# Expert stage's pools in another order in SBUF, and another order of products in the last gated group

## The chip, the core and the metric

The kernel runs on one core of a Trainium2 chip. The metric is the device time of one execution in microseconds (us). Engines are named as the profile names them: PE (TensorE, matmuls), PEld (its weight loads), ACT (ScalarE), DVE (VectorE), POOL (GpSimd) and SP (SyncE, which issues most DMAs). Every engine works through its own list of instructions in order; semaphores hold an instruction until what it needs is there.

## The reference, cut to what matters

Three stages follow each other on 2304 tokens of 512 features.

```
# attention: 4 batches x 8 heads, 576 tokens, head size 64
proj = x @ w_phi;  proj -= max(abs(proj));  phi(x) = [exp(proj), exp(-proj)]
kv, z = phi(k).T @ v, sum(phi(k));  out = (phi(q) @ kv) / (phi(q) @ z + 1e-6)

# experts: each token goes to one of 8
e_idx = argmax(x @ w_gate + modality_bias[modality_id]);  gate_w = softmax value of e_idx
out[mask_e] = gate_w * (relu(x[mask_e] @ w1[e]) @ w2[e])        # 512 -> 1024 -> 512

# gated layer
out = ((x @ w_a) * (x @ w_b)) @ w_out                           # 512 -> 1536 -> 512
```

## The kernel before

All matmuls run on fp32 values split into a high and a low part, three matmuls for each product (`mm3`, lines 53 to 56), so every weight and every input needs a high copy (made by ACT) and a low copy (high subtracted, made by DVE).

**Attention** (class `Attn`) goes through eight pairs of heads (units 0 to 7). Its order on PE is written by hand (`manual_schedule`). Units 0 to 3 are route 0 (half of the tokens), 4 to 7 route 1. Names: `pjp` projections, `df` differences, `qtp` and `qts` turned queries, `kxp` and `kx` key sums, `nmp` numerators, `x` the result, which `store` writes to the DRAM tensors `xs`; `lgp` are the router's logits, added up by POOL (lines 259, 261).

**Routing** (class `Route`, one for each half): gate (`modi` is its first DVE instruction, line 357), rank, place and table. Its products are `idx`, which tells a gather which rows of `xs` belong to which tile (line 504), `perm`, the way back, and `meta`, which expert a tile belongs to. Route 0 is worked out during attention; route 1 waits for unit 7 and runs on DVE beside the first expert tiles.

**Expert stage** (class `Moe`): four tiles of 608 tokens, two from each half (tile 0 and 1 of route 0, tile 2 and 3 of route 1). For a tile POOL issues five gathers (`xg`, line 561, buffers from the pool `m_xg`), PE turns the gathered rows (`mxt`, line 573), ACT and DVE split them (`mxh`, `mxl`, lines 576 and 577, pool `m_xt`). SP loads eight raw weight pieces (`s`, line 544, pool `m_st`), ACT and DVE split each (`wh`, `wl`, lines 552 and 553, pool `m_w`). Then come eight `l1` steps (`hp`, with `hh` and `hl` as the split result, lines 590 and 591) and four `l2` steps (`yp`, copied to `y`, line 603). A tile has 384 matmuls on PE, 192 of `hp` and 192 of `yp`.

**Conversion**: the gated layer's weights come as 64-bit floats. Ten of their twelve pieces are converted beside the expert stage (`prep` and `narrow`, lines 678 to 718): SP loads `raw` (line 685), ACT, POOL (line 690) and DVE (lines 691 to 698 and 707 to 716) turn it into sums and split parts, SP stores them to the DRAM tensors `wsc`. They have a low priority in the scheduler.

**Gated layer** (class `Moe2`): 36 groups, three pairs of token blocks by twelve slices of 128 columns. A group computes seven products `abp` (line 837), which ACT copies to `pc` (line 839), DVE combines and multiplies (`gate`, lines 825 to 829: `ca`, then `gh` by ACT and `gl` by DVE, first for part 0, then for part 1). The output product (`outp`, line 805) of a group is six accumulations `op0` to `op5`, three matmuls each; `op0` to `op2` need part 0 of the gate, `op3` to `op5` part 1. The products of a group are interleaved with the `op` of the group before. After the twelfth slice `finish` (line 785) scales each accumulation to `o` and POOL scatters it to the output (line 797).

What sets the order: in attention and in the gated layer PE's list is written by hand. In the expert stage a scheduler sets every engine's list when the program is built, from its own costs and from when buffers become free. A pool gives its tiles fixed addresses; pools opened with `side="right"` lie one after the other from the right end of SBUF, in the order in which they are opened, and a tile whose address was another tile's before waits for that one's last reader. Attention has two pools there, for the loaded queries and keys (`a_ld`, 18432 bytes of each partition) and for `df` (`a_df`, 20480 bytes left of it). The free part left of them begins 38912 bytes from the right end.

Of the kernel before, what the change touches and what calls it, by code (L numbers as in the profile page):

```python
# [43 lines left out]
XG = 5  # L44
# [4 lines left out]
def f32(ap):  # L49
    return ap.bitcast(F32)  # L50


def mm3(nc, out, lh, ll, rh, rl, start, stop):
    nc.tensor.matmul(out, lh, rh, start=start, stop=False)  # L54
    nc.tensor.matmul(out, lh, rl, start=False, stop=False)  # L55
    nc.tensor.matmul(out, ll, rh, start=False, stop=stop)  # L56


class Attn:
    def __init__(self, nc, tc, ctx, cst, qk, v, vt, xs, lgp):  # L60
        self.nc, self.tc = nc, tc
        self.qk, self.v, self.vt, self.xs = qk, v, vt, xs
        self.cst, self.lgp = cst, lgp
        pool = lambda n, b, **kw: ctx.enter_context(tc.tile_pool(name=n, bufs=b, **kw))
        self.p_ld = pool("a_ld", 2, side="right")
        self.p_df = pool("a_df", 5, side="right")
        self.p_v = pool("a_v", 3)
        self.p_x = pool("a_x", 2)
        self.p_sm = pool("a_sm", 4)
        self.p_kx = pool("a_kx", 2)  # L70
        self.p_qt = pool("a_qt", 11)
        self.p_vt = pool("a_vt", 2)
        self.p_kp = pool("a_kp", 4)
        self.p_kt = pool("a_kt", 3)
        self.ps_p = pool("aps_p", 2, space=PSUM)
        self.ps_q = pool("aps_q", 2, space=PSUM)
        self.ps_c = pool("aps_c", 2, space=PSUM)
        self.u = {}
# [441 lines left out]
class Moe:  # L520
    NJ = 8

    def __init__(self, nc, tc, ctx, cst, xs, wm, y, ps_l, ps_t):
        self.nc, self.tc, self.cst, self.xs, self.wm, self.y = nc, tc, cst, xs, wm, y
        pool = lambda n, b, **kw: ctx.enter_context(tc.tile_pool(name=n, bufs=b, **kw))
        r = dict(side="right", reuse_waits="tile")
        self.p_st = pool("m_st", 2, **r)
        self.p_w = pool("m_w", 3, **r)
        self.p_xg = pool("m_xg", XG, **r)
        self.p_xt = pool("m_xt", 1, **r)  # L530
        self.p_h = pool("m_h", 1, **r)
        self.ps_l, self.ps_t = ps_l, ps_t

# [121 lines left out]
class Moe2:  # L655
# [124 lines left out]
    def run(self, ws, ts, src0, side):  # L780
        nc, n = self.nc, self.N
        seq = [(p, f) for p in range(NTOK // n // 2) for f in range(self.NF)]
        accs, gs = {}, {}

        def finish(p):
            for m, acc in enumerate(accs.pop(p)):
                bp, b = divmod(2 * p + m // 3, HALF // n)
                if m % 3 == 0:
                    os = self.p_o.tile([P, 3, DM], F32, tag="raw", name="o", bufs=2)
                o = os[:, m % 3, :]  # L790
                c = b * (n // P) + m % 3
                g2 = self.routes[bp].g2[:, c:c + 1]
                if m % 2:
                    nc.vector.tensor_scalar(out=o, in0=acc, scalar1=g2, scalar2=None, op0=ALU.mult)
                else:
                    nc.scalar.activation(o, acc, AF.Copy, scale=g2)  # L796
                st = nc.gpsimd.indirect_dma_start(  # L797
                    out=self.out[:, :],
                    out_offset=bass.IndirectOffsetOnAxis(ap=self.routes[bp].perm[:, c:c + 1], axis=0),
                    in_=o, in_offset=None)  # L800
                for other in self.stores:
                    self.tc.declare_no_dep(st.ins, other, reason="each row of the output is stored once")
                self.stores.append(st.ins)

        def outp(k, m):
            p, f = seq[k]
            if f == 0 and m == 0:
                accs[p] = [self.ps_a.tile([P, 512], F32, tag=f"a{i}", name=f"op{i}") for i in range(6)]
            gh, gl = gs[k]
            wh, wl = ws[k](1536, 512)  # L810
            ms = slice(P * (m % 3), P * (m % 3) + P)
            mm3(nc, accs[p][m], gh[:, m // 3, ms], gl[:, m // 3, ms], wh, wl, f == 0, f == self.NF - 1)
            if m == 5:
                del gs[k], ws[k]
                if f == self.NF - 1:
                    finish(p)

        def stage(k):
            p, f = seq[k]
            ct = lambda tag, shape: self.p_c.tile([P] + shape, F32, tag=tag, name=tag)  # L820
            ca, u, d = ct("ca", [2, n]), ct("u", [2, n]), ct("d", [2, n])
            out = []
            gs[k] = [self.p_g.tile([P, 2, n], F32R, tag=t, name=t) for t in ("gh", "gl")]

            def gate(i, other):
                gh, gl = (x[:, i, :] for x in gs[k])
                nc.vector.tensor_mul(ca[:, i, :], ca[:, i, :], other)  # L827
                nc.scalar.copy(gh, ca[:, i, :])  # L828
                nc.vector.tensor_sub(gl, ca[:, i, :], f32(gh))  # L829

            for i, (col, t) in enumerate(self.PROD):
                ps = self.ps_l.tile([P, 512], F32, tag="l", name="abp")[:, :n]
                wh, wl = ws[k](col, 256)
                th, tl = ts[p][t]
                for c in range(2):
                    cs = slice(P * c, P * c + P)
                    mm3(nc, ps, wh[:, cs], wl[:, cs], th[:, c, :], tl[:, c, :], c == 0, c == 1)
                x = self.p_c.tile([P, n], F32, tag="pc", name="pc", bufs=5)
                nc.scalar.copy(x, ps)  # L839
                out.append(x)  # L840
                if i == 1:
                    nc.vector.tensor_add(u[:, 0, :], x, out[0])
                elif i == 2:
                    nc.vector.tensor_add(ca[:, 0, :], x, out[0])
                elif i == 3:
                    nc.vector.tensor_add(u[:, 1, :], x, u[:, 0, :])
                elif i == 4:
                    nc.vector.tensor_add(d, u, x.unsqueeze(1).to_broadcast([P, 2, n]))  # L848
                elif i == 5:
                    nc.vector.tensor_add(x, x, u[:, 1, :])  # L850
                    gate(0, x)
                elif i == 6:
                    nc.vector.tensor_add(ca[:, 1, :], x, d[:, 0, :])
                    gate(1, d[:, 1, :])
                if k and i > 1:
                    for m in (i - 2,) if i < 6 else (4, 5):
                        outp(k - 1, m)

        src = src0
        self.rest(src, ts[0])  # L860
        for k, (p, f) in enumerate(seq):
            with self.tc.high_priority(offset=-LOWP2):
                for st in side.get(k, ()):
                    st()
            if k + 1 < len(seq) and k + 1 not in ws:
                ws[k + 1] = self.weights(k + 1)
            if f == 0 and p:
                self.rest(src, ts[p])
            with self.tc.manual_schedule(engines={mybir.EngineType.PE}):
                stage(k)  # L870
            if f == self.NF - 2 and k + 2 < len(seq):
                src, ts[p + 1] = self.terms(p + 1, self.p_s)
        with self.tc.manual_schedule(engines={mybir.EngineType.PE}):
            for m in range(6):
                outp(len(seq) - 1, m)


def low(tc, step):
# [171 lines left out]
```

## Time and profile before

| what | value |
|---|---|
| three timed runs | 839.76, 842.74 and 843.46 us |
| the profiled execution | 840.43 us, of which the span from first to last instruction is 838.6 us |
| PE busy | 802.0 us, 96% of the span |
| DVE busy | 595.5 us, 71% |
| ACT busy | 375.1 us, 45% |
| POOL busy | 134.1 us, 16% |
| granted TensorE clock, mean | 0.991 of full speed |

A busy share is a mean over the whole run: attention lasts until about 169 us, the expert stage until about 406 us, and the gated layer from there to the end. The rows below are from single stretches. In a row of the timeline the first number is the start and the second the duration in us; in brackets stands how long the engine had been idle before, and what ended that.

### The profile page before, as it was taken

To read this page: it belongs to the slowest core of one execution; us is meant where nothing else is said; L and a number is where in the kernel's file an instruction comes from. 1 tells how busy PE (TensorE), PEld (TensorE's weight loads), DVE (VectorE), ACT (ScalarE), POOL (GpSimd) and SP (SyncE) were. 2 spreads that over 40 slices of the span, in tenths; PEclk is the share of its full clock that TensorE was granted. 3 is DMA by queue.
4 is the path that set the end of the run, shared out by engine and by line. 5 is a ranking of instruction groups with operands and counts; after the bars stand their busy time and mean duration, and the time that the engine had idled before them with its cause. 6 is when DMAs were issued, how large, how long until landed. Compare 5 with 4: busy or idle time off the path is not lost.

```text
span 838.6 us, 18331 instructions
## 1 busy us (share of the span) xinstructions
PE 802.0 (96%) x7284; PEld 752.8 (90%) x7284; DVE 595.5 (71%) x1071; ACT 375.1 (45%) x665; POOL 134.1 (16%) x164
## 2 busy tenths in 40 slices
PE   9999998899989999989899999999999999999995
PEld 7989888899989999989889899989999999999994
DVE  6877998689995989797588855675554476545553
ACT  4555555434452555444445433553333364333332
POOL 1000018433233522510031000020000002000002
PEclk9999999999998999999999999999999999999998
DMA  8755431667668888776689876576666668666631
GB/s 300 221 173 165 161 90 31 215 217 275 225 202 283 295 303 295 239 288 251 230 286 332 280 241 201 195 257 214 225 202 199 192 201 301 202 203 201 190 135 75
DMA packets 85163, 184.22 MB, mean 220 GB/s; under 512 B 27760, under 2 KB 37520, under 8 KB 85072
## 3 DMA queue, kind: packets, MB, share of 16 engines
q1 hardware_dynamic: 81872, 173.21, 61.6%
q0 software_dynamic: 3040, 9.72, 3.2%
q8 instruction: 58, 0.95, 0.5%
q14 instruction: 33, 0.27, 0.1%
q10 hardware_dynamic: 160, 0.07, 0.0%
HBM read 145.21 MB, written 37.75 MB: 218 GB/s over the span
## 4 chain that ended last, share of the span: by engine, by line
PE 24%; issue 19%; DVE 4%; POOL 2%; ACT 2%; DMA 1%; POOLq 0%; DVEq 0%; ACTq 0%
PE abp L54 5%; PE abp L56 5%; PE abp L55 5%; PE op L56 3%; PE op L55 3%; PE op L54 3%; POOL cvs L690 1%; DMA wsc<-whi 1%; POOL out L797 1%; ACT pc L839 1%; DVE gl L829 0%; DVE d L848 0%; ACT yh L744 0%; DVE ca L827 0%; DVE yl L745 0%
## 5 line engine op out<-in xcount | busy, mean ns | idle before, releaser
L839 ACT COPY pc<-abp 128x384 f32<-128x384 f32 x252 | 120.5, 479 | 199.3 <-PE abp L56 194.2
L54 PE MATMUL abp<-yh,fw 128*128 128x384 f32 x504 | 169.9, 337 | 3.2 <-ACT pc L839 2.2
L55 PE MATMUL abp<-yl,fw 128*128 128x384 f32 x504 | 169.9, 337 | 0.0
L56 PE MATMUL abp<-yh,fw 128*128 128x384 f32 x504 | 169.9, 337 | 0.0
L54 PEld LDWEIGHTS abp<-yh,fw 128*128 128x128 f32 x504 | 94.6, 188 | 13.1 <-ACT pc L839 4.0
L55 PEld LDWEIGHTS abp<-yl,fw 128*128 128x128 f32 x504 | 94.6, 188 | 7.6
L690 POOL TENSOR_SCALAR cvs<-cvs 128x768 f32<-128x768 f32 x24 | 62.7, 2612 | 210.5 <-ACT cvs L689 158.3
L56 PEld LDWEIGHTS abp<-yh,fw 128*128 128x128 f32 x504 | 94.6, 188 | 0.0
L54 PE MATMUL op<-fw,gh 128*128 128x512 f32 x216 | 85.4, 395 | 1.0 <-ACT gh L828 1.0
L56 PE MATMUL op<-fw,gl 128*128 128x512 f32 x216 | 85.3, 395 | 0.9 <-DVE gl L829 0.9
L55 PE MATMUL op<-fw,gh 128*128 128x512 f32 x216 | 85.4, 395 | 0.0
L54 PE MATMUL hp<-mxh,wh 128*128 128x304 f32 x256 | 78.8, 309 | 3.7 <-DVE hl L591 3.7
L55 PE MATMUL yp<-hl,wh 128*128 128x304 f32 x256 | 77.1, 302 | 1.0 <-DVE hl L591 1.0
L55 PE MATMUL hp<-mxl,wh 128*128 128x304 f32 x256 | 77.9, 305 | 0.0
L56 PE MATMUL yp<-hh,wl 128*128 128x304 f32 x256 | 77.7, 304 | 0.0
L56 PE MATMUL hp<-mxh,wl 128*128 128x304 f32 x256 | 77.7, 304 | 0.0
L54 PE MATMUL yp<-hh,wh 128*128 128x304 f32 x256 | 76.7, 303 | 0.5 <-ACT y L603 0.5
L797 POOL DMA_INDIRECT out<-o,perm x18 | 18.1, 1006 | 355.9 <-ACT o L796 349.4
L190 ACT ACTIVATE qts<-qtp 128x512 f32<-128x512 f32 (+1 forms) x80 | 38.3, 557 | 57.2 <-PE qtp L187 57.2
L848 DVE TENSOR_TENSOR d<-u,pc 128x768 f32<-128x768 f32 x36 | 34.4, 956 | 33.9 <-ACT pc L839 33.7
L54 PEld LDWEIGHTS hp<-mxh,wh 128*128 128x128 f32 x256 | 48.7, 191 | 4.9 <-DVE hl L591 2.8
L828 ACT CAST gh<-ca 128x384 fp32r<-128x384 f32 x72 | 36.9, 515 | 34.6 <-DVE ca L827 34.6
(191 smaller groups left out, 1584.4 us busy)
## 6 DMA issues: line engine op xcount, KB each, us to landing
fw<-wsc SPq DMA_DIRECT2D x72, 512.0 KB, 3.6
fw<-wsc SPq DMA_DIRECT2D x144, 256.0 KB, 3.3
raw<-in_moe_w SPq DMA_DIRECT2D x24, 768.0 KB, 6.2
s<-in_moe_w SPq DMA_DIRECT2D x32, 512.0 KB, 5.8
fw<-wsc SPq DMA_DIRECT2D x72, 128.0 KB, 2.6
wsc<-whi SPq DMA_DIRECT2D x12, 640.0 KB, 4.8
wsc<-wsum SPq DMA_DIRECT2D x12, 640.0 KB, 5.0
wsc<-whi SPq DMA_DIRECT2D x12, 512.0 KB, 4.2
```

Source lines behind the costliest of these rows:

```text
L54: nc.tensor.matmul(out, lh, rh, start=start, stop=False)
L55: nc.tensor.matmul(out, lh, rl, start=False, stop=False)
L56: nc.tensor.matmul(out, ll, rh, start=False, stop=stop)
L190: nc.scalar.activation(t[:, s, :n, :], ps[:, :n, :], AF.Exp, scale=1.0 - 2.0 * s)
L690: nc.gpsimd.tensor_scalar(out=s.bitcast(F32), in0=s.bitcast(F32), scalar1=LEAST, scalar2=None, op0=ALU.max)
L797: st = nc.gpsimd.indirect_dma_start(out=self.out[:, :], out_offset=bass.IndirectOffsetOnAxis(ap=self.routes[bp].perm[:, c:c + 1], axis=0), ...
L828: nc.scalar.copy(gh, ca[:, i, :])
L839: nc.scalar.copy(x, ps)
L848: nc.vector.tensor_add(d, u, x.unsqueeze(1).to_broadcast([P, 2, n]))
```

## The change

The first part opens the pools of the expert stage in another order. Bytes from the right end of SBUF, before: `m_st` 0 to 8192, `m_w` to 32768, `m_xg` to 43008, `m_xt` to 62464. Now: `m_w` 0 to 24576, `m_xt` to 44032, `m_xg` to 54272, `m_st` to 62464. So the gather buffers and the raw weights lie in the free part, and the split inputs lie partly where `df` was.

The second part concerns the last of the 36 groups alone: all its seven products are computed without an `op` between them, product 5 ahead of product 4, and then the twelve `op` of the last two groups follow in the order written.

```diff
         r = dict(side="right", reuse_waits="tile")
+        self.p_w = pool("m_w", 3, **r)
+        self.p_xt = pool("m_xt", 1, **r)
+        self.p_xg = pool("m_xg", XG, **r)
         self.p_st = pool("m_st", 2, **r)
-        self.p_w = pool("m_w", 3, **r)
-        self.p_xg = pool("m_xg", XG, **r)
-        self.p_xt = pool("m_xt", 1, **r)
         self.p_h = pool("m_h", 1, **r)
...
-            for i, (col, t) in enumerate(self.PROD):
+            last = k + 1 == len(seq)
+            for i in (0, 1, 2, 3, 5, 4, 6) if last else range(7):
+                col, t = self.PROD[i]
...
-                if k and i > 1:
+                if k and i > 1 and not last:
                     for m in (i - 2,) if i < 6 else (4, 5):
                         outp(k - 1, m)
...
                 stage(k)
+                if k + 1 == len(seq):
+                    for back, m in ((1, 0), (1, 1), (1, 2), (0, 0), (0, 1), (0, 2), (1, 3), (0, 3), (1, 4), (0, 4), (1, 5), (0, 5)):
+                        outp(k - back, m)
...
-        with self.tc.manual_schedule(engines={mybir.EngineType.PE}):
-            for m in range(6):
-                outp(len(seq) - 1, m)
```

The scheduler makes other lists of it on every engine of the expert stage. First place: POOL where attention ends. `xs_63` is route 0's half of the attention result, `idx_2633` its row numbers, `lgp_96` the logits of route 1. Before:

```order
L261 TENSOR_TENSOR lgp_96<-lgp_96,x 128x72
L259 TENSOR_TENSOR lgp_96<-lgp_96,x 128x72
L261 TENSOR_TENSOR lgp_96<-lgp_96,x 128x72
L561 DMA xg<-xs_63,idx_2633 128x512 x4
L561 DMA xg<-xs_63,idx_2633 96x512
L303 IOTA i_3184 128x128
```

Now:

```order
L261 TENSOR_TENSOR lgp_96<-lgp_96,x 128x72
L561 DMA xg<-xs_63,idx_2633 128x512 x4
L561 DMA xg<-xs_63,idx_2633 96x512
L259 TENSOR_TENSOR lgp_96<-lgp_96,x 128x72
L261 TENSOR_TENSOR lgp_96<-lgp_96,x 128x72
L561 DMA xg<-xs_63,idx_2633 128x512 x2
L303 IOTA i_3184 128x128
```

The five gathers of tile 0 now stand ahead of two additions that wait for unit 6. The same place on PE, before:

```order
L211 MATMUL kxp<-v,kt 64x73 x2
L231 MATMUL nmp<-kx,qts 64x73 x32
L187 MATMUL qtp<-ident,df 128x128 x8
...
L211 MATMUL kxp<-v,kt 64x73 x2
L573 MATMUL mxt<-ident,xg 128x128 x8
L231 MATMUL nmp<-kx,qts 64x73 x40
L573 MATMUL mxt<-ident,xg 128x128 x8
L573 MATMUL mxt<-ident,xg 128x96 x4
L54 MATMUL hp<-mxh,wh 128x304
```

Now:

```order
L211 MATMUL kxp<-v,kt 64x73 x2
L573 MATMUL mxt<-ident,xg 128x128 x8
L231 MATMUL nmp<-kx,qts 64x73 x32
L187 MATMUL qtp<-ident,df 128x128 x8
...
L211 MATMUL kxp<-v,kt 64x73 x2
L573 MATMUL mxt<-ident,xg 128x128 x4
L231 MATMUL nmp<-kx,qts 64x73 x40
L573 MATMUL mxt<-ident,xg 128x128 x4
L573 MATMUL mxt<-ident,xg 128x96 x4
L54 MATMUL hp<-mxh,wh 128x304
```

The first eight transposes of tile 0 stand one block of `nmp`, `qtp` and `kxp` earlier, and four more follow ahead of the last `nmp`. On SP the first two weight loads of the stage (`s`) now stand ahead of the stores of units 5 and 6 (before: behind those of unit 6). On ACT `mxh` of the first two blocks now follows the first `wh` (before: the second); on DVE the order is now `wl`, `mxl`, `kx`, `mxl`.

Second place: DVE ahead of route 1's `idx_3959`, on which tile 2 depends. Before:

```order
L503 TENSOR_SCALAR tk<-tbp 128x45
L698 TENSOR_TENSOR wsum<-cvt,cvs 128x768
L591 SCALAR_TENSOR_TENSOR hl<-hp,hh 128x608
L691 TENSOR_SCALAR cvt<-cvs 128x768
L708 TENSOR_TENSOR wsum<-wsum 128x256
L709 TENSOR_TENSOR wsum<-wsum 128x256
L483 TENSOR_TENSOR lhs<-i_3184,cl 128x1152
L493 TENSOR_TENSOR tbqr<-tbqh,tokp 128x9x9 x2
L945 TENSOR_TENSOR top<-meta_2204,meta_3720 1x1
L504 TENSOR_TENSOR idx_3959<-tk,tbp 128x45
```

Now:

```order
L503 TENSOR_SCALAR tk<-tbp 128x45
L464 CAST meta_3720<-meta 1x28
L710 TENSOR_TENSOR wsum<-wsum 128x256
L553 TENSOR_TENSOR wl<-s,wh 128x1024
L591 SCALAR_TENSOR_TENSOR hl<-hp,hh 128x608
L693 SCALAR_TENSOR_TENSOR cvt<-raw,cvt 128x768
L483 TENSOR_TENSOR lhs<-i_3184,cl 128x1152
L493 TENSOR_TENSOR tbqr<-tbqh,tokp 128x9x9 x2
L504 TENSOR_TENSOR idx_3959<-tk,tbp 128x45
```

From `modi` of route 1 to this `idx` DVE's list holds 148 instructions before and 151 now: one `wl`, one `hl`, one L693 and one L710 more, and `top` fewer. On PE 528 `hp` and `yp` matmuls stood ahead of tile 2's first `mxt`, and 552 stand there now: the 24 of one more `l1` step of tile 1. POOL's list there is the same in both: nine conversions (L690) and then the gathers of tile 2.

Third place: ACT in the last gated group. Before:

```order
L839 COPY pc<-abp 128x384 x7
L828 CAST gh<-ca 128x384 x2
L796 ACTIVATE o<-op_16900,g_3960 128x512
L796 ACTIVATE o<-op_16902,g_3960 128x512
L796 ACTIVATE o<-op_16904,g_3960 128x512
```

Now:

```order
L841 COPY pc<-abp 128x384 x6
L828 CAST gh<-ca 128x384
L841 COPY pc<-abp 128x384
L828 CAST gh<-ca 128x384
L796 ACTIVATE o<-op_16900,g_3960 128x512
L796 ACTIVATE o<-op_16902,g_3960 128x512
L796 ACTIVATE o<-op_16904,g_3960 128x512
```

The first `gh` stands ahead of the last `pc`; `o` still stands behind both `gh`. `op_16900` to `op_16905` are the accumulations `op0` to `op5`.

## Rows read from the trace of the kernel before

**Rows 1.** Timeline of PE where attention ends, 153 to 170 us
```profile
153.48 2.25 PE L231 MATMUL nmp<-kx,qts 128*64 128x73 f32 x64 [0.76 <-DVE kx L217]
...
160.53 0.35 PE L211 MATMUL kxp<-v,kt 128*64 128x73 f32 x4 [1.85 <-issue]
...
163.12 3.70 PE L231 MATMUL nmp<-kx,qts 128*64 128x73 f32 x80
...
168.90 0.55 PE L573 MATMUL mxt<-ident,xg 96*128 96x96 f32 x4 [1.05 <-DVE mxl L577]
169.23 0.39 PE L54 MATMUL hp<-mxh,wh 128*128 128x304 f32 x1
```

**Rows 2.** Busy time by stretch: start:end, length, engines (instructions), granted clock, DMA share, GB/s
```profile
160.00:165.00 5.00, 4.47 (x62) 4.06 (x63) 3.84 (x8) 2.42 (x4) 2.08 (x2) 0.67 0.77 222
...
200.00:230.00 30.00, 29.01 (x211) 28.76 (x212) 29.92 (x67) 12.36 (x20) 7.73 (x3) 1.00 0.70 244
...
255.00:260.00 5.00, 5.00 (x30) 5.00 (x30) 0.11 (x1) 0.82 (x2) 1.67 (x2) 0.77 0.87 306
```

**Rows 3.** Timelines of POOL and DVE in the same stretch
```profile
142.31 0.35 POOL L261 TENSOR_TENSOR lgp<-lgp,x 128x72 f32<-128x72 f32 x1
...
151.97 1.11 POOL L561 DMA_INDIRECT xg<-xs,idx  x1 [0.61 <-DMA xs<-x]
...
171.95 0.34 POOL L261 TENSOR_TENSOR lgp<-lgp,x 128x72 f32<-128x72 f32 x1
...
172.32 0.17 DVE L357 SCALAR_TENSOR_TENSOR modi<-lgp,modi 128x9 int32<-128x9 int32 x1 [1.77 <-POOL lgp L261]
```

**Rows 4.** Timelines of DVE, POOL and PE where tile 2 begins
```profile
244.06 0.18 DVE L504 TENSOR_TENSOR idx<-tk,tbp 128x45 int32<-128x45 f32 x1
...
245.74 2.96 POOL L690 TENSOR_SCALAR cvs<-cvs 128x768 f32<-128x768 f32 x1 [5.35 <-ACT cvs L689]
248.85 1.34 POOL L561 DMA_INDIRECT xg<-xs,idx  x1 [0.16 <-issue]
...
253.37 1.09 PE L573 MATMUL mxt<-ident,xg 128*128 128x128 f32 x4 [5.22 <-DMA xg<-xs,idx]
...
259.89 0.79 DVE L591 SCALAR_TENSOR_TENSOR hl<-hp,hh 128x608 fp32r<-128x608 f32 x1 [5.21 <-ACT hh L590]
...
271.54 0.60 PE L573 MATMUL mxt<-ident,xg 128*128 128x128 f32 x4
```

**Rows 5.** Groups of DVE instructions by shape: count, busy us, mean ns, idle before
```profile
L553 DVE TENSOR_TENSOR wl<-s,wh 128x1024 fp32r<-128x1024 f32 x32 | 40.0, 1249 | 3.5 <-ACT wh L552 3.4
...
L591 DVE SCALAR_TENSOR_TENSOR hl<-hp,hh 128x608 fp32r<-128x608 f32 x32 | 24.9, 779 | 10.2 <-ACT hh L590 10.2
...
L693 DVE SCALAR_TENSOR_TENSOR cvt<-raw,cvt 128x768 int32<-128x768 int32 x24 | 22.7, 947 | 0.0
```

**Rows 6.** Timeline of PE: one wait for `hl`, and two matmuls in a row
```profile
204.58 0.41 PE L55 MATMUL yp<-hl,wh 128*128 128x304 f32 x1 [0.99 <-DVE hl L591]
...
405.16 0.30 PE L54 MATMUL yp<-hh,wh 128*128 128x304 f32 x1
405.30 0.30 PE L55 MATMUL yp<-hl,wh 128*128 128x304 f32 x1
```

**Rows 7.** Timelines of SP and PE where the expert stage ends
```profile
387.14 22.42 SPq L727 DMA_DIRECT2D fw<-wsc  x16
...
406.76 0.45 PE L54 MATMUL abp<-yh,fw 128*128 128x384 f32 x1 [1.03 <-ACTq L978]
```

**Rows 8.** Timelines of PE and POOL at the end of the run
```profile
828.04 0.39 PE L56 MATMUL op<-fw,gl 128*128 128x512 f32 x1
...
828.72 0.39 PE L56 MATMUL op<-fw,gl 128*128 128x512 f32 x1
...
827.00 0.97 POOL L797 DMA_INDIRECT out<-o,perm  x1 [126.31 <-ACT o L796]
...
833.37 0.97 POOL L797 DMA_INDIRECT out<-o,perm  x1 [0.30 <-issue]
```

## The prediction

> **What bounds the kernel now.** The page's first part comes first: PE is busy 96% of the span and every other engine has room. So what the change can win lies where PE is idle, where its granted clock is low, or after its last matmul; I went to these places in the timeline. There are three, and DVE, the next busiest engine, decides whether what they give is kept.
>
> Where attention ends, PE waits 0.76 for `kx`, then stands 1.85 at "issue", and 1.05 for `mxl` before the last transposes of tile 0 [rows 1]. The stretch from 160 to 165 is granted 0.67 of the clock [rows 2]; the 80 `nmp` there take 3.70, against 2.25 for 64 (2.8 for 80) a little before [rows 1]. POOL meanwhile: its first gather of tile 0 goes out at 151.97, behind additions that wait for unit 6, although POOL had finished the addition ahead of them at 142.7 [rows 3].
>
> Where tile 2 begins, PE is idle for 5.22, ended by the gather: `idx` was ready at 244.06, POOL finished a conversion at 248.70 before it issued the gather, and 4.52 later (253.37 less 248.85) PE starts [rows 4]. PE arrived at 253.37 less 5.22 = 248.15. Then it is slow: 255 to 260 runs at 0.77 [rows 2].
>
> At the end, six scatters leave POOL one by one, 1.27 apart (827.00 to 833.37 in five steps); the profiled span ends at 838.6, so POOL's chain, not PE's last matmul at 829.1, is what ends last [rows 8].
>
> DVE is busy 29.92 of 30.00 from 200 to 230 [rows 2], while PE waits for `hl` there once, 0.99 [rows 6].
>
> **The change part by part.** All of this is against the profiled time, 840.43.
>
> *Start of the expert stage.* The five gathers of tile 0 move from 151.97 to right behind the addition at 142.31 [rows 3], 1.27 apart as the scatters at the end [rows 8]; with the 4.52 of the gather at tile 2 [rows 4] the first two land by 142.7 + 1.3 + 4.5 = 148.5. The eight transposes that need them then fill the 0.76 gap, and four more stand ahead of the last `nmp`. The wait of 0.76 goes. Behind the last `nmp` eight transposes are left, not twelve (4 x 0.14 = 0.6 less), and the 1.05 wait for `mxl` should mostly go, since three of the five `mxl` now come earlier. That makes the first `hp` 0.76 + 0.6 + 1.05, or about 2.2 earlier than 169.23 where the pieces overlap. But twelve matmuls later (about 170.9) an accumulator is needed that the evictions of the last `nmp` free, and DVE now has a third `wl` (1.25 [rows 5]) ahead of them. I put the lead at 1.4, between 0.2 (that `wl` in the way) and 3.7 (below). Route 1's `modi` hangs on POOL's last addition (171.95), which is itself behind gathers [rows 3]; two of five gathers now go earlier, and I take 2.1 for it.
>
> A place for the rule on the clock: a 0.76 and a 1.85 gap were followed by 0.67 here [rows 1, 2], and a 5.22 gap by 0.77 [rows 2, 4]. [...]
>
> *Tile 2.* Three things meet. Route 1's `idx`: DVE has 151 instructions from `modi` to it and not 148: a `wl` (1.25), an `hl` (0.78), an L693 (0.95) more [rows 5] and an L710 (a third of L693's columns, so 0.3) more; less a short one and the overlap of their starts I take 3.0. So 244.06 - 2.1 + 3.0 = 245.0. POOL: its nine conversions are in the list as before, but the ninth began at 245.74 for a late ACT input [rows 4]; with that input one DVE step earlier it should be done by about 245, and the gather goes out at 245.2 and lands at 245.2 + 4.52 = 249.7. PE: it has 24 more matmuls ahead of this point. At 0.14 each [rows 6] it arrives at 248.15 - 1.4 + 3.4 = 250.1. So the wait goes to about nothing, and with it the low clock. The second transposes for tile 2 stand 90 matmuls on: 250.1 + 0.6 + 90 x 0.14 = 263.3, where before it was 271.54 [rows 4], a lead of 8.2. In parts this is 1.4 from the start, 5.22 of wait, and 1.6 of clock (18.17 from 253.37 to 271.54, where 114 matmuls at 0.14 and one transpose of 0.6 are 16.6).
>
> The rule on the gather: the row says 4.52 from issue to PE's start [rows 4]. [...]
>
> *What is late next.* With PE 8 earlier, DVE has to keep up. Before tile 2's first `hl` it was idle for 5.21 [rows 4]; that was the cover, and the change uses it up. DVE's extra 3.0 is work that the old order did later, so it is not lost, but from there to the end of tile 3 DVE is about as late as PE. I give back 0.9 of the 8.2 (one wait like the 0.99 [rows 6]), which leaves 7.3. The bounds are nothing given back, and everything but the start's 1.4. At the end of the stage the weights for the gated layer (`fw`) are issued from 387.14, and PE began on them at 406.76 [rows 7]; with PE at 399.5 there are 12 us between, so this costs nothing; if it had no cover it would be up to 7.
>
> *The tail.* Of the last group, `op0` now has eight `op` behind it and had five. An `op` takes 0.68 (828.72 less 828.04 [rows 8]), so the first result is ready 3 x 0.68 = 2.04 before its old time against PE's end. On ACT the second `gh` and the last `pc`, which stood between, are done long before; that is worth up to 0.4. PE's amount of work is unchanged. The first three results come 0.68 apart and the rest every 1.36 (two `op`), so the scatters, 1.27 apart, have a stock to draw on: the sixth `op` ends with PE at 829.1, and its scatter's turn is only 2.2 before 833.37, at about 831.2. The gain is 2.2, between 1.5 and 2.6.
>
> Sum: 840.43 - 7.3 - 2.2 = 830.9. The median of the runs shown, 842.74, lies 2.3 above the profiled execution; I take half of this, +1.1, hence 832.0.
>
> **The rivals.** *DVE has no slack*: every us that PE gains in tile 2 is waited out again at `hl` before tile 3 ends. For it: 29.92 of 30.00 [rows 2]. Against it: with DVE that full PE waited once. What stays is 1.4 + 2.2: 836.8, 838.0 at the median's level.
>
> *The start gives more*: PE's clock stays up and the evictions come in time, a lead of 3.7. For it: the filled gap. Against it: the 1.85 stays. PE would then wait at tile 2 for the gather, but all of it would come earlier; the lead at 271.54 is then some 9.5, nothing is given back: 840.43 - 9.5 - 2.2 = 828.7, 829.9 at the median's level. [...]
>
> *Slower*: DVE's new order puts a `wl`, an L693 or a piece of route work right ahead of the `hl` that PE needs, and each of the 16 `hl` of tiles 2 and 3 costs PE a wait of 0.99 [rows 6]. That is 15.8, against 9.5 gained: 846.7, 847.9 at the median's level. It decides from the tenth such wait (9.9 over 9.5). For it: DVE is full, and its order was set by a scheduler with costs of its own. Against it: DVE's idle time ahead of `hl` sums to 10.2 over all 32 [rows 5], so `hl` is mostly early.
>
> *The first part doesn't do what it says*: the gathers go out early but land with the stores and weights of attention's end, so that nothing before `hp` moves; and the new `idx` is later by as much as PE. Only the tail stays: 838.2, 839.4 at the median's level.
>
> **How the numbers follow.** 0.5% of 842.74 is 4.2 us, so faster means under 838.5 and slower over 846.9; less a measurement of this kernel cannot tell from no change. Forecast 0.50, no slack 0.25, more at the start 0.12, slower 0.07, nothing but the tail 0.06. Faster is the forecast, the third case, and half of the second (838.0 lies right at the bound): 0.50 + 0.12 + 0.13 = 0.75. Same is the other half, the last case and a little of the slower one: 0.20. Slower is 0.05. The forecast's own range is 829 to 835 (start 0.2 to 3.7, tail 1.5 to 2.6, the level of the runs 0 to 2.3); the whole range takes in the second and third case and ends short of the slower one: 827 to 840.
>
> **What would show it.** Right: POOL's first five `xg` near 143; first `hp` at 167 to 168; no idle time over 1 us before tile 2's first transposes and granted clock 1.00 in the 15 us after it; the second transposes of tile 2 near 263; `abp` starting near 399.5; the first scatter 6.3 us before the last one still, but starting while PE has over 4 us to go. Wrong: waits for `hl` of about 1 us in a row in tiles 2 and 3; `idx` of route 1 after 247, so that PE waits for the gather as before; a first `abp` at 405 or later; DVE idle for less than 2 us between 250 and 380 with PE waiting for it.

## The result, and the profile after

| | before | after |
|---|---|---|
| median of the timed runs | 840.23 us (837.85 to 843.46, six runs) | 831.11 us (829.97 to 834.64, six runs) |
| span of the profiled execution | 838.6 | 830.2 |
| granted clock, mean | 0.991 | 0.996 |

The ratio is 0.9903, with a 95% interval of 0.9877 to 0.9928. The forecast was 832.0, and the time is inside its own range. The gain is 9.1 us against the median beside it, where the forecast had 10.7 against the median that it knew (842.74); the two repeats below gave 5.9 and 8.1. The places where the time came from are not the ones that I had named, though. I follow PE through the profile after and set it against [rows 1 to 8].

Timeline of PE where attention ends, after (as in rows 1: start, duration, in brackets the idle time before and what ended it):

```profile
153.49 1.09 PE L573 MATMUL mxt<-ident,xg 128*128 128x128 f32 x8
...
162.35 0.66 PE L573 MATMUL mxt<-ident,xg 128*128 128x128 f32 x4 [1.88 <-DVE mxl L577]
162.97 2.76 PE L231 MATMUL nmp<-kx,qts 128*64 128x73 f32 x80
165.66 0.99 PE L573 MATMUL mxt<-ident,xg 128*128 128x128 f32 x8
166.43 0.38 PE L54 MATMUL hp<-mxh,wh 128*128 128x304 f32 x1
...
169.40 0.37 PE L54 MATMUL hp<-mxh,wh 128*128 128x304 f32 x1 [0.91 <-DVE x L242]
```

The eight early transposes fill the gap of 0.76, and the 1.05 for `mxl` is gone. But a new wait of 1.88 stands ahead of the transposes of the third block of rows, and 0.91 ahead of the fourteenth `hp`. The 80 `nmp` took 2.76, not the 3.70 of [rows 1].

Timeline of DVE, after:

```profile
160.47 1.23 DVE L553 TENSOR_TENSOR wl<-s,wh 128x1024 fp32r<-128x1024 f32 x1 [2.80 <-ACT wh L552]
161.61 0.68 DVE L577 TENSOR_TENSOR mxl<-mxt,mxh 128x512 fp32r<-128x512 f32 x1
...
170.32 0.17 DVE L357 SCALAR_TENSOR_TENSOR modi<-lgp,modi 128x9 int32<-128x9 int32 x1 [0.61 <-POOL lgp L261]
...
175.64 0.56 DVE L691 TENSOR_SCALAR cvt<-cvs 128x768 int32<-128x768 int32 x1 [1.85 <-POOL cvs L690]
...
206.06 1.50 DVE L716 TENSOR_TENSOR wsum<-wsum,whi 128x1280 fp32r<-128x1280 f32 x1 [1.10 <-ACT whi L715]
...
248.65 0.19 DVE L504 TENSOR_TENSOR idx<-tk,tbp 128x45 int32<-128x45 f32 x1
```

The 1.88 is in the first two rows: `mxl`, which frees the transposes' accumulator, stands behind a `wl` that waited 2.80 for its `wh`. `modi` is 2.0 earlier than in [rows 3], but `idx` is 4.6 later than in [rows 4]. DVE's wait of 1.85 for `cvs` goes back to a load. ACT in the kernel before, then ACT and POOL after:

```profile
172.38 0.90 ACT L689 ACTIVATE cvs<-raw 128x768 f32<-128x768 f32 x1 [2.41 <-DMA raw<-in_moe_w]
```

```profile
172.47 0.90 ACT L689 ACTIVATE cvs<-raw 128x768 f32<-128x768 f32 x1 [5.15 <-DMA raw<-in_moe_w]
173.46 2.14 POOL L690 TENSOR_SCALAR cvs<-cvs 128x768 f32<-128x768 f32 x1 [3.17 <-ACT cvs L689]
```

POOL waited 3.17 for ACT, and ACT 5.15 for the load of `raw`, which let it begin no earlier than before.

The lead at the first `hp` does not last until tile 2. PE at the 505th of the 1536 `hp` and `yp` matmuls of the stage, before, and then after, with the largest wait ahead of it:

```profile
244.40 0.30 PE L54 MATMUL hp<-mxh,wh 128*128 128x304 f32 x1
```

```profile
217.58 0.41 PE L56 MATMUL yp<-hh,wl 128*128 128x304 f32 x1 [1.08 <-DVE wl L553]
...
244.95 0.30 PE L54 MATMUL hp<-mxh,wh 128*128 128x304 f32 x1
```

There the new order is 0.55 behind.

Timelines of POOL and PE where tile 2 begins, after:

```profile
242.45 2.13 POOL L690 TENSOR_SCALAR cvs<-cvs 128x768 f32<-128x768 f32 x1 [2.86 <-ACT cvs L689]
249.58 2.67 POOL L561 DMA_INDIRECT xg<-xs,idx  x1 [5.00 <-DMA s<-in_moe_w]
252.56 1.54 POOL L561 DMA_INDIRECT xg<-xs,idx  x1 [0.30 <-issue]
254.40 3.60 POOL L561 DMA_INDIRECT xg<-xs,idx  x1 [0.30 <-issue]
258.30 0.94 POOL L561 DMA_INDIRECT xg<-xs,idx  x1 [0.30 <-issue]
...
256.30 0.94 PE L573 MATMUL mxt<-ident,xg 128*128 128x128 f32 x4 [4.26 <-DMA xg<-xs,idx]
...
270.93 0.60 PE L573 MATMUL mxt<-ident,xg 128*128 128x128 f32 x4
```

The conversion is out of the way, as forecast (POOL is idle for 5.00), but PE still waits 4.26. The second transposes of tile 2 stand at 270.93, where [rows 4] had 271.54: by here the change has won 0.6. Busy time by stretch, after (columns as in rows 2), shows the low clock behind the wait:

```profile
250.00:255.00 5.00, 2.05 (x22) 1.85 (x21) 5.00 (x8) 1.86 (x3) 4.39 (x3) 1.00 0.56 179
255.00:260.00 5.00, 3.70 (x16) 3.70 (x17) 4.38 (x7) 0.00 (x0) 4.39 (x3) 0.66 0.92 294
```

Groups of PE instructions from 165 to 415 (count, busy us, mean ns, idle before and what ended it), before and then after:

```profile
L54 PE MATMUL hp<-mxh,wh 128*128 128x304 f32 x256 | 78.8, 309 | 3.7 <-DVE hl L591 3.7
```

```profile
L54 PE MATMUL hp<-mxh,wh 128*128 128x304 f32 x256 | 78.8, 308 | 1.9 <-DVE hl L591 0.9 <-DVE x L242 0.9
```

In the kernel before, the 3.7 are five waits for `hl` (0.17, 0.90, 0.74, 1.11, 0.78) in tiles 2 and 3, from 298 to 372. After, none is there: the 0.9 are three small ones before 190. Each of the five also cost more than its idle time, by 0.24 to 0.27. One of them, PE, before:

```profile
357.81 0.30 PE L56 MATMUL hp<-mxh,wl 128*128 128x304 f32 x1
358.86 0.41 PE L54 MATMUL hp<-mxh,wh 128*128 128x304 f32 x1 [0.74 <-DVE hl L591]
359.10 0.30 PE L55 MATMUL hp<-mxl,wh 128*128 128x304 f32 x1
```

In a row without a wait the starts are 0.14 apart [rows 6]; here they are 1.05 and 0.24, together 1.01 more, for 0.74 of idle time. The end, PE, then POOL, after:

```profile
401.54 0.45 PE L54 MATMUL abp<-yh,fw 128*128 128x384 f32 x1 [1.02 <-ACTq L980]
...
822.75 0.40 PE L56 MATMUL op<-fw,gl 128*128 128x512 f32 x1
```

```profile
818.58 0.96 POOL L797 DMA_INDIRECT out<-o,perm  x1 [123.87 <-ACT o L796]
...
824.95 0.97 POOL L797 DMA_INDIRECT out<-o,perm  x1 [0.31 <-issue]
```

Against [rows 7] the gated layer starts 5.22 earlier; against [rows 8] PE ends 5.96 earlier and the last scatter starts 8.42 earlier. So the 8.4 of the span are 0.6 up to the second transposes of tile 2, 4.6 from there to the gated layer, 0.7 in the gated layer and 2.4 behind PE's last matmul.

### The profile page after: what moved, and what is told of

The parts are those of the page before. It is cut to its first block, busy times and chain, and to the rows that moved or that the text cites. A ratio compares the mean times of both kernels' runs of the same rounds, so it can differ in the third digit from the quotient of the medians.

```text
span 830.2 us, 18334 instructions
## 1 busy us (share of the span) xinstructions
PE 800.1 (96%) x7283; PEld 752.1 (91%) x7284; DVE 597.2 (72%) x1071; ACT 375.7 (45%) x665; POOL 136.3 (16%) x164
## 4 chain that ended last, share of the span: by engine, by line
PE 30%; issue 16%; DVE 2%; ACT 1%; DMA 1%; POOL 0%; POOLq 0%; SPq 0%; DVEq 0%; ACTq 0%
PE abp L54 6%; PE abp L56 6%; PE abp L55 6%; PE op L56 4%; PE op L55 4%; PE op L54 4%; DMA wsc<-whi 1%; POOL out L797 0%; DVE ca L827 0%; ACT pc L841 0%; DVE gl L829 0%; ACT yh L744 0%; DVE d L850 0%; DVE yl L745 0%; DVE ca L855 0%
## 5 line engine op out<-in xcount | busy, mean ns | idle before, releaser
L690 POOL TENSOR_SCALAR cvs<-cvs 128x768 f32<-128x768 f32 x24 | 61.7, 2573 | 196.2 <-ACT cvs L689 147.6
L552 ACT CAST wh<-s 128x1024 fp32r<-128x1024 f32 x32 | 33.6, 1050 | 42.6 <-PE hp L55 24.4
```

Of the source, the lines that this page charges most:

```text
L552: nc.scalar.copy(hi, src)
L690: nc.gpsimd.tensor_scalar(out=s.bitcast(F32), in0=s.bitcast(F32), scalar1=LEAST, scalar2=None, op0=ALU.max)
```

## The experiments

The table cuts each profile at three places: the first `hp`, the first `abp`, and PE's end. The ratio is to the kernel before that ran beside it on the same chip: e1 to e4 shared one, e5 to e8 another, e9 to e11 a third, and e12 ran on a fourth.

| kernel | first `hp` | `hp` to `abp` | `abp` to PE's end | behind it | ratio to before (95%) |
|---|---|---|---|---|---|
| before | 169.23 | 237.5 | 422.4 | 9.49 | |
| after | 166.43 | 235.1 | 421.6 | 7.05 | 0.9903 (0.9877 to 0.9928) |
| e1_tail | 171.81 | 236.9 | 422.3 | 7.05 | 0.9970 (0.9951 to 0.9988) |
| e2_pools | 173.49 | 236.0 | 421.7 | 9.57 | 0.9965 (0.9941 to 0.9989) |
| e3_xg | 170.00 | 235.1 | 421.6 | 7.12 | 0.9913 (0.9886 to 0.9941) |
| e4_st | 174.41 | 237.8 | 422.4 | 7.09 | 0.9952 (0.9932 to 0.9972) |
| e5_after | 169.93 | 235.1 | 421.9 | 7.10 | 0.9938 (0.9914 to 0.9962) |
| e6_order | 176.71 | 232.6 | 421.9 | 9.26 | 0.9947 (0.9918 to 0.9976) |
| e7_route | 171.52 | 233.4 | 422.1 | 7.08 | 0.9904 (0.9872 to 0.9936) |
| e8_rhigh | 176.35 | 229.0 | 421.7 | 7.07 | 0.9898 (0.9858 to 0.9938) |
| e9_after | 166.37 | 235.5 | 421.8 | 7.02 | 0.9900 (0.9866 to 0.9933) |
| e10_mxl | 164.11 | 235.9 | 421.6 | 7.11 | 0.9878 (0.9836 to 0.9920) |
| e11_both | 164.57 | 234.0 | 423.5 | 7.07 | 0.9882 (0.9836 to 0.9927) |
| e12_nine | 171.24 | 233.1 | 423.4 | 7.10 | 0.9886 (0.9869 to 0.9902) |

Each row is one execution, and `hp` to `abp` can depend on when the first `hp` came: e6_order has the list of the kernel after up to the last group, started `hp` 6.8 later than e5_after on the same chip, and took 232.6 where that took 235.1. So 2 or 3 in this column alone say little. A narrower cut says more. From the second transposes of tile 2 (behind 642 `hp` and `yp` in all nine) to the first `abp`, the six kernels with the expert stage of the kernel after (after, e2, e3, e5, e6, e9) take 130.60 to 130.61, and the three with that of the kernel before (before, e1, e4) take 134.01 to 135.23.

**One part at a time.** e1_tail is the kernel after with the pools of before; e2_pools the kernel before with the new pools.

> The pools stay as before; only the last gated group is in the new order. Theory (the tail gains by itself: PE ends 5.96 us earlier in the profile after, the span 8.4, so 2.4 lies behind PE's last matmul): 2.4 us less than the kernel before, ratio about 0.997, the time from PE's last matmul to the end of the span 7.05 and not 9.49. Rival (the scatters are held by something else when the rest is late): no difference, 9.5 again.

> Only the pools are in the new order; the last gated group is as before. Theory (the two parts add up): about 6 us less than the kernel before, ratio 0.993, PE at the first product of the gated layer near 401.5, and 9.5 us from PE's last matmul to the end. Rival (the parts overlap): the ratio is that of the kernel after, 0.990.

The tail did as its theory said: 0.3% is 2.5 of the 844.45 that the kernel before took beside it, and 7.05 stand behind PE's end. e2_pools gave 3.0, not 6, though the sum of the two is still inside the interval of e5_after. In its profile `hp` to `abp` (236.0) and from there to PE's end (421.7) are near the kernel after; what is missing is ahead of the first `hp`.

**One pool at a time.** Both are the kernel after with one pool put back; the order of the pools from the right end:

```
 e3_xg: m_st, m_w, m_xt, m_xg        e4_st: m_w, m_xg, m_xt, m_st
```

> Both parts, but the raw weights (m_st) stay at the right end, where the queries and keys of attention lie; only the gather buffers go to the free part. Every engine's list is that of the kernel after, save SP's, where the first two weight loads stand behind the stores of unit 6. Theory (the gather buffers alone make the scheduler's new lists, and these do the work): within 1.5 us of the kernel after, 831. Rival (the early weight loads matter at the start: the first wl is late without them): the first hp is 1 to 3 us later than 166.4 and the whole run 2 us or more slower than the kernel after.

> Both parts, but the gather buffers (m_xg) lie where attention's df was, so only the raw weights are in the free part. Every engine's list is that of the kernel before with the new tail, save SP's. Theory (the gather buffers do the work): 2.4 us less than before from the tail and nothing more, 838, with the wait of about 5 at tile 2 and the five waits for hl (0.17 to 1.11) still there. Rival (early raw weights give the start lead): 1 to 2 us less than that.

e3_xg missed the 831 (836.54), and its first `hp` is 3.6 later than 166.4, where its rival had 1 to 3; but e5_after, the kernel after itself, came to 837.55 and a first `hp` as late. In the stage itself e3_xg is the kernel after, so the early weight loads are worth nothing that can be seen there. e4_st has the wait at tile 2 and three of the five waits for `hl` in tiles 2 and 3 (0.90, 1.22, 0.79). So the place of the gather buffers makes the new lists. By its ratio e4_st is 4.0 faster than before, not 2.4, which is what its rival said; its first `hp` (174.41) shows no early start, and its interval (2.4 to 5.7) reaches down to the tail alone, so this stays open. Timeline of PE in e4_st:

```profile
259.20 1.09 PE L573 MATMUL mxt<-ident,xg 128*128 128x128 f32 x4 [4.79 <-DMA xg<-xs,idx]
...
365.54 0.41 PE L54 MATMUL hp<-mxh,wh 128*128 128x304 f32 x1 [1.22 <-DVE hl L591]
```

**Is the start part of it?** e5_after and e9_after are the kernel after, unchanged.

> The kernel after once more, on the chip of this study beside the kernel before. Theory (its parts add up: last group 2.5, expert stage 2.0 and gated layer 0.7 shorter in every profile with the new gather buffers, while the time at which the first hp starts differs by up to 7 between kernels that are the same up to there): about 5 to 7 us less than before, ratio 0.992 to 0.994, and a first hp anywhere from 166 to 174. Rival (the start lead of 2.8 in the first profile belongs to the change): ratio 0.990 again, and a first hp within 1 of 166.4.

> The kernel after for a third time, as the measure of the two runs that follow it on the same chip. Ratio to before between 0.990 and 0.994; 1.88 of wait for mxl ahead of the third transpose of tile 0 and 4 to 4.6 of wait at tile 2, as in all its profiles.

Kernels whose lists are the same up to the first `hp` (after, e2, e3, e5, e6, e9) reach it anywhere from 166.37 to 176.71; those with the lists of before (before, e1, e4) from 169.23 to 174.41. So the 2.8 of the first pair of profiles cannot be put down to the change. e9_after has the ratio and the first `hp` of the first profile again, as the rival of e5_after had it, and e5_after has neither. The place varies on one chip too: e5_after and e6_order, with the same list up to there, were profiled on the same chip and are 6.8 apart. Timeline of PE in e2_pools shows one source, gaps at "issue" in `nmp` while tile 0's gathers run, and the other, the clock (granted 0.78 from 170 to 175):

```profile
149.17 0.39 PE L231 MATMUL nmp<-kx,qts 128*64 128x73 f32 x5 [0.40 <-issue]
150.62 1.01 PE L231 MATMUL nmp<-kx,qts 128*64 128x73 f32 x25 [1.05 <-issue]
...
167.78 0.66 PE L573 MATMUL mxt<-ident,xg 128*128 128x128 f32 x4 [1.88 <-DVE mxl L577]
168.39 4.39 PE L231 MATMUL nmp<-kx,qts 128*64 128x73 f32 x80
```

The 1.88 is there in each kernel with the new list (1.87 in e9_after). It is the change's own; with the old list PE waits 1.05 to 2.11 for `mxl` ahead of the last transposes instead.

**The order of the last `op`.** All seven products first, but `op0` to `op5` of group 34 and then those of group 35:

```diff
-for back, m in ((1, 0), (1, 1), (1, 2), (0, 0), (0, 1), (0, 2), (1, 3), (0, 3), ...
+for back, m in ((1, 0), (1, 1), (1, 2), (1, 3), (1, 4), (1, 5), (0, 0), (0, 1), ...
```

> As the kernel after, but the last twelve op stand in the order op0 to op5 of the group before and then op0 to op5 of the last; the seven products still come first. Theory (the gain of the last group is that op0 of the last group has eight op behind it and not five): the first scatter starts 2.1 to 2.5 before PE's end and the span ends 9.1 to 9.5 after it, as in the kernel before; 2 us slower than the kernel after. Rival (the gain is that the gate of the last group is ready early, so nothing waits there): the tail stays at 7.1 and the time is that of the kernel after.

Timelines of PE and POOL at its end:

```profile
830.85 0.39 PE L56 MATMUL op<-fw,gl 128*128 128x512 f32 x1
...
828.81 0.97 POOL L797 DMA_INDIRECT out<-o,perm  x1 [125.96 <-ACT o L796]
```

The first scatter leaves 2.43 before PE's end (2.11 before, 4.57 after), and 9.26 stand behind it. So the mechanism is shown: it is the place of `op0`, not the early products. Its whole time against e5_after (840.26 against 837.55) agrees, but the intervals overlap, and its first `hp` was late.

**An earlier `idx`.** The routing steps of the second half get another priority:

```diff
-        side = {k: [low(tc, rs[f])] for f, k in enumerate((0, 3, 5, 8))}
+        side = {k: [rs[f]] for f, k in enumerate((0, 3, 5, 8))}             # e7_route
+        side = {k: [high(tc, rs[f])] for f, k in enumerate((0, 3, 5, 8))}   # e8_rhigh
```

> As the kernel after, but the routing of the second half has the priority of the expert stage in the scheduler and not a lower one: on DVE 136 instructions from modi to idx and not 148 (9.2 us less by the durations of the profile after), on POOL eight conversions ahead of tile 2's gathers and not nine. Theory (the wait of 4.26 for tile 2's gather and the low clock behind it, about 1.6, are still paid in the kernel after because idx is late on DVE): no wait over 1 at tile 2, granted clock 1.00 there, 5 to 6 us less than the kernel after, ratio about 0.985. Rival (DVE has no slack: what is put behind idx makes hl late in tiles 2 and 3): waits for hl of 0.9 to 1.1 come back three to five times, and the time is within 2 us of the kernel after.

> As the run before, but the routing of the second half has a higher priority than the expert stage: 131 instructions on DVE from modi to idx (14 us less than in the kernel after), six conversions on POOL ahead of the gathers. Theory (idx is what tile 2 waits for): no wait at tile 2; as little time as the run before, within 1.5. Rival (wl and hl of tiles 0 and 1 now stand behind the routing): waits for hl or wl of 1 us or more in tiles 0 and 1 from 175 on, and no gain over the kernel after.

PE where tile 2 begins, e7_route and then e8_rhigh:

```profile
253.99 0.55 PE L573 MATMUL mxt<-ident,xg 128*128 128x128 f32 x3 [1.68 <-DMA xg<-xs,idx]
...
301.28 0.41 PE L54 MATMUL hp<-mxh,wh 128*128 128x304 f32 x1 [1.98 <-ACT y L603]
```

```profile
248.36 0.63 PE L573 MATMUL mxt<-ident,xg 128*128 128x128 f32 x4 [0.75 <-DMA xg<-xs,idx]
```

The wait shrinks from 4.5 to 1.68 and 0.75, and the granted clock is 1.00 in each stretch of 5 us from 240 to 270. So a late `idx` had a large part in it. It is not moved alone here: the first transposes of tile 2 also stand earlier on PE (behind 528 and 456 `hp` and `yp`, not 552), and in e8_rhigh the gather still took 6.80 from issue to PE (241.56 to 248.36). The time did not follow in full: both medians (834.61, 834.41) are 3 below e5_after's 837.55, not 5 to 6, with intervals that overlap, and in these profiles the first `abp` comes at 404.93 and 405.39, no earlier than e5_after's 405.04, after a first `hp` that is 1.6 and 6.4 later. Other waits came instead: in e7_route 0.76 for `hl` at 209 and 1.98 for `y` at 301, in e8_rhigh 1.53 for `hl` at 213, of the kind that its rival named.

**The 1.88 taken away.** The first split moves behind two transposes; e11_both adds e8's priority:

```diff
-        split(0)
         for j in range(NSUB):
             self.transp(Ts[0], j)
+            if j == 1:
+                split(0)
```

> As the kernel after, but the first split of the raw weights is written behind the first two transposes of tile 0 and not ahead of them: on DVE both mxl now stand ahead of the first wl, and the third wl behind the evictions (x) of the last nmp. It also makes the scheduler's later lists anew: 136 instructions from modi to idx and seven conversions on POOL ahead of tile 2's gathers. Theory (the early gathers gain little at the start because the third transpose of tile 0 waits 1.88 for an accumulator whose mxl stands behind wl, and x behind another wl): the waits of 1.88 and 0.9 go, so from the end of the last kxp (about 160.3 in the kernel after) to the first hp it is 4.3 and not 6.2; with an earlier idx (tile 2's wait under 1) 5 us or more less than the kernel after, ratio about 0.986. Rival (the first wl is what the first hp waits for): the wait comes back ahead of the first hp, and only tile 2 gains.

> As the run before, with the routing of the second half at a higher priority as well: 129 instructions from modi to idx, six conversions on POOL ahead of tile 2's gathers. Theory (start and idx are two separate costs): no wait at tile 2 and no 1.88 at the start; expert stage 229 from the first hp to the first product of the gated layer, as with the priority alone, and 6 to 8 us less than the kernel after, ratio 0.984. Rival (DVE is the bound once both are gone): waits for hl in tiles 0 and 1 that add up to 3 or more, no better than the run before.

Timeline of PE in e10_mxl:

```profile
159.31 1.25 PE L573 MATMUL mxt<-ident,xg 128*128 128x128 f32 x8 [0.29 <-DVE mxl L577]
...
164.11 0.38 PE L54 MATMUL hp<-mxh,wh 128*128 128x304 f32 x1
...
168.16 0.55 PE L54 MATMUL hp<-mxh,wh 128*128 128x304 f32 x2 [2.13 <-ACT mxh L576]
...
276.85 0.41 PE L54 MATMUL yp<-hh,wh 128*128 128x304 f32 x1 [2.33 <-ACT y L603]
...
356.33 0.38 PE L54 MATMUL hp<-mxh,wh 128*128 128x304 f32 x1 [2.49 <-DVE hl L591]
```

The first `hp` is 2.3 earlier than in e9_after (5.1 behind the last `kxp`, where 4.3 was expected and e9_after has 5.95). But a wait comes back at the thirteenth `hp`, for `mxh`, and longer (2.13, where e9_after waits 0.98 for `x` at the fourteenth). At tile 2 PE no longer waits and the clock stays up (granted 1.00 in each stretch of 5 us from 240 to 270), which should be worth the 4.65 of e9_after and more; yet `hp` to `abp` is not shorter (235.9 against 235.5), since 2.33, 1.00 and 2.49 are waited out later, for `y` and `hl`. That fits neither the theory nor its rival: the start gained a little, and the gain at tile 2 did not last.

e11_both missed its expectation at tile 2. Timelines of POOL and PE:

```profile
230.51 3.04 POOL L561 DMA_INDIRECT xg<-xs,idx  x1 [12.38 <-DVE idx L504]
233.85 3.94 POOL L561 DMA_INDIRECT xg<-xs,idx  x1 [0.31 <-issue]
...
241.74 0.66 PE L573 MATMUL mxt<-ident,xg 128*128 128x128 f32 x4 [1.86 <-DMA xg<-xs,idx]
```

Its `idx` comes 60.5 after `modi` (67.5 in e7_route, 78.3 in the kernel after), yet PE waits 1.86 for the gather, which took 11.2 from issue to PE: an early `idx` alone is not enough. `hp` to `abp` is 234.0 and not 229, and the waits for `hl` in tile 0 (1.08 and 1.54) come near the 3 of the rival. The six runs of e10_mxl (828.61 to 830.95) lie 1.3 lower in the median than those of e9_after (829.60 to 833.91), and e11_both 1.8 lower, where the expectation was 5 to 8. They are the fastest kernels run, by an amount that the intervals do not separate from the kernel after.

**Less work beside the expert stage.** `NPRE = 9` in place of 10, in e10_mxl.

> As the run with the first split behind the first two transposes, but nine of the gated layer's twelve weight pieces are converted beside the expert stage and not ten (three, not two, beside the gated layer, where DVE is busy some 55%). It takes about a tenth of the conversion off DVE and POOL; the lists up to tile 2 are the same. Theory (PE's waits of 1.00 and 2.49 for hl at tiles 2 and 3, which took the place of the wait at tile 2, come from DVE's amount of work): they shrink to under 1 together, 2 to 3 us less, ratio 0.984 to 0.986. Rival (they come from the order in which the scheduler put the work, not from its amount): waits of 2 or more for hl or y are still there, and the ratio stays at 0.988.

The wait for `hl` in tile 3 fell from 2.49 to 0.93, which would fit DVE's amount of work; but 1.39 came for `hl` in tile 0, `y` still costs 1.97 and 0.83, and the ratio stayed at 0.989, near what the rival said. The expert stage is shorter (233.1 against 235.9, with a first `hp` 7.1 later) and the gated layer longer (423.4 against 421.6). That the third conversion in the gated layer is what it pays for is not shown: e11_both converts ten pieces ahead of it and takes 423.5.

## Why the prediction was right, and where it was not

The time came out right because two steps were wrong in opposite ways. The forecast had 8.2 at tile 2, 0.9 given back, and 2.2 at the tail. Measured were 0.6, 4.6 and 0.7 *gained* after it, and 2.4. That the sums are so near (9.5 and 8.4) is luck.

*Start.* "I put the lead at 1.4." At the fourteenth `hp` the first profile shows 171.13 less 169.40, or 1.7, but the spread over like kernels says that no number of this size can be read from one pair. Nor was a lead kept up to tile 2, as "248.15 - 1.4 + 3.4 = 250.1" has it: PE arrived at 252.04. The premise that the 1.85 gap stays was wrong too: no other profile has it. The step named the third `wl` ahead of the evictions rightly (the 0.91), and missed that the early transposes would be held up: their accumulators are freed by `mxl`, and the new order of DVE puts a `wl` ahead of it.

*Tile 2, the step that failed: "244.06 - 2.1 + 3.0 = 245.0".* `idx` came at 248.65. The 2.0 at `modi` and the extra instructions are there. But I moved the whole of DVE's list earlier with `modi`, and its next conversion needs POOL, which began it at 173.46, as late as in the kernel before (173.37), since both hang on the load of `raw`. Between `modi` and `idx` DVE was idle for 4.4 (0.43, 1.85, 0.83, 0.19, 1.10, each ended by POOL or ACT), against 0.27 before. With 3.0 of instructions that makes 7.1, and `modi` to `idx` is 6.6 longer (78.3 against 71.7). This is the larger part of the error, not all of it. The forecast had the gather landed at 249.7, and PE began on it at 256.30. Of these 6.6, 3.65 are `idx`, 0.7 is the way from `idx` to the gather (0.93, where 0.2 was allowed) and 2.2 the gather itself. With `idx` on time but this gather PE would have waited about 0.6, and with the gather of 4.52 but this `idx` about 2.1.

*The gather's 4.52* became 6.7 (249.58 to 256.30). POOL's part of it grew from 1.34 to 2.67, which is 1.3 of the 2.2; the rest, and the 6.80 of e8_rhigh, where POOL's part was 1.04, stay open. The next two gathers took POOL 1.54 and 3.60. What makes the three long is not shown. DVE was busy throughout them (2.67 of 2.67 us, 1.54 of 1.54, 3.60 of 3.60), but also throughout the next, which took 0.94 (at 258.30), and the third of the kernel before, which took 0.95 (at 252.10); so a busy DVE alone is not it. Busy time there, as in rows 2, before:

```profile
252.10:253.05 0.95, 0.00 (x0) 0.00 (x0) 0.95 (x3) 0.00 (x0) 0.94 (x1) 0.50 0.96 272
```

The kernels with the same lists as the kernel after repeat its 2.67, 1.54 and 3.60 to within 0.01. So the lengths come with the lists, and no run here shows by which instructions.

*"What is late next"* had the wrong sign. I let DVE, once full, cost PE 0.9 of waits; in fact the new order put the `hl` of tiles 2 and 3 where PE no longer waits for them at all, for 3.7. e3 and e4 show that this comes with the gather buffers' place, through the scheduler's list. It cannot be had from timing the parts that the diff names. The other 0.9 of the 4.6 is in the main what the five waits cost beyond their idle time, 0.24 to 0.27 each; the 0.9 that I gave back for one wait left this out. The 0.7 in the gated layer, which the kernels with the new gather buffers have but for e7, e11 and e12, was not forecast. It has come about in the first 85 us of that layer, and its cause stays open.

*Tail.* 2.2 forecast, 2.44 measured (9.49 less 7.05), by the mechanism named.

*The rivals.* The fourth (the first part does little) was nearest up to tile 2, where only 0.6 had been won; behind it, it was wrong by the 4.6. In the first profile the clock stayed up at the start, as the second rival had it (1.00 from 160 to 175, 80 `nmp` in 2.76), but e2_pools and e6_order have 4.39 with the same list and the same wait of 1.88 ahead of it, so it is not the change's, and no run shows by how much a gap lowers the clock behind it; its lead of 3.7 and its 9.5 stand without a working. "DVE has no slack" did not show here, but e10 to e12, whose lists differ in more than this, point to it as soon as tile 2's wait is taken away: then what is won is waited out again.

## What to carry to other kernels

Where a scheduler orders the lists, a buffer's address is an edit of every list, and the gain can lie a hundred us from the edit: compare waits stage by stage before crediting one. When a chain of instructions starts earlier, ask for every instruction in it that also needs another engine whether that engine starts earlier too. Where results leave one by one, the first should be ready as early before the last matmul as the order allows: here 4.57 ahead of it left 7.05 to drain, and 2.43 left 9.26.

## What was not expected

The same instructions take up to 10 us more or less to the first `hp` (166.37 to 176.71), on one chip up to 6.8. Seen in it are gaps at "issue" (2.2 in `nmp` around 147 to 151 in e2, none in the profile after) and the granted clock (0.78 from 170 to 175 in e2, where the 80 `nmp` took 4.39; 1.00 in the profile after, where they took 2.76). In e2 the gaps stand where the gathers of tile 0 are issued, but the kernel after issues them at the same time without such gaps, so their cause is open.
